# The row of D in a fused SSM-convolution and SwiGLU kernel: loaded through GpSimd's DMA queue instead of SyncE's

## The chip, the cores and the metric

One NeuronCore of a Trainium2 chip runs the whole kernel. The metric is the device time of one execution in microseconds (us), as the median of several. A profiled execution of the same program gives the trace; its times are microseconds from the start of the span unless marked otherwise. The engines are PE (TensorE, with PEld for its weight loads), DVE (VectorE), ACT (ScalarE), POOL (GpSimd) and SP (SyncE, which here only issues transfers). "SPq" marks the instruction that issues a transfer on SP's queue; transfers issued by POOL show as POOL instructions, since GpSimd spends its own time on them.

## The reference

The input has 2048 rows of 640 numbers. Two layers follow each other, both with a residual:

```python
kv = (sum of 4 shifted copies of k, each times a column of shift_k) * v
y  = causal convolution of kv with ssm_k, per channel (done by FFT of 2*S)
y  = y + kv * ssm_D
h  = x + layernorm(x) * y
h2 = h + (silu(n @ w_gate) * (n @ w_up)) @ w_down,   n = layernorm(h)
```

`ssm_D` is one row of 640 numbers. The product `kv * ssm_D` is the same as adding `ssm_D` to the first tap of the convolution kernel `ssm_k`, and so the kernel adds this row once, to one row of the first block of `ssm_k`.

## The kernel before

The sequence is cut into four blocks of 512 rows. For each block j the kernel does, in names that the code uses: load g (a block of `ssm_k`), k, v and x; turn g on PE (L471) and evict the result (L473); multiply the shifted k on PE (block 0: L639, the later blocks: L648) and multiply with v (kv); take the spectra X (of kv) and G (of g) by matmuls with the constant WF (L375), each result copied out of PSUM by ACT (L364) or DVE (L367) and completed by one subtraction on DVE (L410); multiply spectra on DVE (block 0: L719, stage "m00"); go back by an inverse transform (L878); multiply with the layernorm of x and add x (L892, L905); normalise, turn (hT) and run the feed-forward part (gate and up: L1022, down: L1110).

Nothing is left to a scheduler at run time. The function records every operation with its engine and its buffers in a `Plan`, and the list `ORDER` gives the order in which the recorded operations are written out; each number is the index of an operation, and a negative number `n` means operation `~n` on its other engine (a copy on DVE instead of ACT, or a load issued by POOL, called "pld", instead of SP). Each engine then runs its own operations in that order, and waits at each for what it needs. Buffers come from a few pools and are handed out in the same order (12 of "big", 5 of "row", 4 of "ps", which are the PSUM tiles). The list was made by a planner that is not part of the kernel.

The operations that matter for the change, with their numbers in `ORDER`:

- 22, 29, 26, 27, 28 and 205 are the first loads, all on SP: k (L597), g of block 0 (L330), x (L342), v (L337), WF (L1199), x of block 1 (L342). Each is 512 or 640 KB. Operation 31 is the load of the row of D (L1208), 1280 bytes into partition 0 of a "row" buffer; it is the seventh transfer on SP's queue.
- 63 is the addition of that row to the turned g, on DVE (L477). It stands in `g_turned`, behind the four evictions of the turned g (56, 58, 60, 62; L473). Operation 62 is the fourth of these.
- 44, 47 and 53 (L658) multiply three of the four products of k with v on DVE; 50 (ACT, L664) and 51 (DVE, L665) do it for the fourth.
- 64 to 97 are the spectrum X of block 0, in two halves of the columns; its pairs of matmuls are the even numbers 64, 66, ..., and their evictions the odd ones. 98 to 129 are G of block 0, which alone needs the sum made by operation 63. 142 is the first multiplication of m00.
- 13 (POOL, L1170) rearranges the taps once these have landed, 12 (POOL, L1166) writes one fifth of the diagonals for the product with k, 24 (POOL, L1189) clears a tail.
- 614 is a copy of the shifted k of block 3 inside SBUF (L563), issued by POOL. 533 is a load of weights for block 1's feed-forward part (L959). 290, 293, 296 and 299 are transfers by which POOL adds the four rows of block 1's result into x (L278). 307 is the last of the four normalisations of block 1 (L807), behind which the last transpose by DMA (L919) is issued.

Of the kernel before, what the change touches and what calls it, by code (L numbers as in the profile page):

```python
# [68 lines left out]
TW = PAD + BLK  # L69
CUTS = ("X0", "G0", "m", "i")  # L70
ORDER = [
# [36 lines left out]
SLOTS = {'S': 8, 'big': 12, 'kT': 0, 'tT': 1, 'row': 5, 'sg': 0, 'co': 2, 'ps': 4, 'sm': 6}  # L108
HOME = {t: "big" for t in ("scr", "x", "ld", "t4", "hT", "wgu", "diag")} | {"o": "row", "ps_c": "ps", "ps_f": "ps"}
SPLIT = ((0,), (1,))  # L110
# [102 lines left out]
def kernel(ctx: ExitStack, tc: tile.TileContext, A_q, A_k, A_v, A_shift_k, A_ssm_k, A_ssm_D, B_x,  # L213
          B_w_gate, B_w_up, B_w_down, out):
    nc = tc.nc
# [15 lines left out]
    plan = Plan(slots)  # L231

    def new(tag):
        return Buf(HOME.get(tag, tag), None, tag)
# [7 lines left out]
    def ap(b):  # L242
        if b.tag != "big":
            return b.ap if b.tag is None else place[b.tag][b.at]
        t = place["big"][b.at]
        return t if b.kind == "ld" else t.rearrange("p (k n) -> p k n", k=KT if b.kind in ("hT", "wgu") else 4 * KT if b.kind == "diag" else R)
# [17 lines left out]
    def load(nbytes, packet, fn, w, r=(), other=None):  # L264
        op = plan.moved("sp", nbytes, packet, fn, r, w)
        if other:
            op.other = ("pld", op.ns, other)
        return op
# [864 lines left out]
    def first(name):  # L1133
        plan.line(0, name)
# [70 lines left out]
        load(P * R * 4 * P * 2, 4096, lambda: nc.sync.dma_start(out=ap(minus)[:, 0:4, :], in_=minus_h.ap()), [minus])  # L1205
    first("Ld")
    drow = new("row")
    load(1280, 1280, lambda: nc.sync.dma_start(out=ap(drow)[0:1, :], in_=A_ssm_D.partition_broadcast(1)), [drow])  # L1208
    first("LWI")
    load(P * R * 4 * P * 2, 4096, lambda: nc.sync.dma_start(out=ap(WI), in_=wi_h.ap()), [WI])  # L1210

# [26 lines left out]
    for j in range(1, NB):  # L1238
# [4 lines left out]
        if j == 1:  # L1243
            stage("Lw")
            load(P * NC_FULL * D * 2, 1280, lambda: nc.sync.dma_start(
                out=ap(wd)[:, 0:NC_FULL, :], in_=B_w_down[0:NC_FULL * P, :].rearrange("(c p) d -> p c d", p=P)), [(wd, 0)])
# [84 lines left out]
```

## Time and profile before

| | |
|---|---|
| time, median of 3 runs | 263.84 us (263.32 to 264.68) |
| time of the profiled execution | 265.31 us |
| its span in the trace | 263.5 us |
| PE busy | 254.7 us (97%) |
| DVE, ACT, POOL busy | 201.3, 180.8, 96.3 us |
| transfers | 45.05 MB, 63505 packets |

The profiled execution took 265.31 us, of which the trace spans 263.5; the rest lies ahead of and behind the first and last instruction. The trace is read in four views: the page with its slices, the chain of waits (which work ended last, followed back), the waits themselves (who waited for whom), and the timeline, in which each row is a start, a duration, an engine, a line of the code, an operation with its tiles, and in brackets the idle time ahead of it with what ended it. A row with "xN" merges N instructions in sequence. The table of stretches gives each engine's busy time in a stretch, and the clock that PE was granted there, as a share of the full one.

### The profile page before, as it was taken

The page shows a single profiled execution, that of the slowest core. Times are in us where ns is not written, and L with a number is a line of the kernel's source. Part 1 is how long each engine was busy: PE and PEld are TensorE (multiplying, and loading weights), DVE is VectorE, ACT ScalarE, POOL GpSimd, SP SyncE. Part 2 cuts the span into 40 slices and gives each one's busy share as a digit, 9 for nine tenths or more (in the row PEclk, how much of TensorE's full clock was granted, in tenths as well). Part 3 has the DMA queues.
Part 4 walks back from the last instruction along what each step waited for, and adds up shares of the span by engine and source line. Part 5 has one row for each costly group of instructions (what it writes and reads, how often), then busy time and mean ns, then how long its engine had stood idle before and what let it go on. Part 6 is the DMA issues. An engine that isn't in the chain of part 4 may idle for free.

```text
span 263.5 us, 4713 instructions
## 1 busy us (share of the span) xinstructions
PE 254.7 (97%) x1818; PEld 155.7 (59%) x1818; DVE 201.3 (76%) x263; ACT 180.8 (69%) x295; POOL 96.3 (37%) x115
## 2 busy tenths in 40 slices
PE   8979989999999999999999999999999999999993
PEld 7946658654566467764465467544446764444662
DVE  4388999999999999999999999999998300002231
ACT  2858999999999896889877879174677035345100
POOL 6923900003932952582017790407942022000000
PEclk9989999999999999999999999999999999999999
DMA  6997979978998999996997957765869557000011
GB/s 212 397 256 182 256 158 346 212 189 243 248 284 126 147 215 209 197 200 136 230 239 156 243 131 149 150 102 124 187 199 279 92 149 96 0 0 0 2 50 50
DMA packets 63505, 45.05 MB, mean 171 GB/s; under 512 B 30966, under 2 KB 58940, under 8 KB 63484
## 3 DMA queue, kind: packets, MB, share of 16 engines
q1 hardware_dynamic: 57586, 32.30, 49.2%
q0 software_dynamic: 5888, 12.46, 25.2%
q8 instruction: 14, 0.23, 0.4%
q14 instruction: 7, 0.06, 0.1%
q10 hardware_dynamic: 10, 0.01, 0.0%
HBM read 30.01 MB, written 4.59 MB: 131 GB/s over the span
## 4 chain that ended last, share of the span: by engine, by line
PE 81%; DVE 9%; DMA 3%; ACT 3%; SPq 1%; issue 1%; DVEq 0%
PE ps L1022 44%; PE ps L1110 23%; PE ps L375 8%; PE ps L878 4%; DMA row<-in_A_ssm_D_dram 3%; DVE S L719 2%; PE ps L648 2%; ACT big L364 1%; DVE row L892 1%; DVE big L658 1%; DVE big L719 1%; ACT S L364 1%; SPq L342 1%; DVE big L823 1%; DVE S L367 0%
## 5 line engine op out<-in xcount | busy, mean ns | idle before, releaser
L1022 PE MATMUL ps<-big,big 128*128 128x512 bf16 x540 | 120.5, 379 | 0.0
L1022 PEld LDWEIGHTS <-big 128*128 128x128 bf16 x540 | 52.4, 98 | 59.7
L1110 PE MATMUL ps<-wd,tT 128*128 128x320 bf16 (+2 forms) x416 | 60.9, 299 | 0.6 <-DVE row L1127 0.6
L1110 PEld LDWEIGHTS <-tT 128*128 128x128 bf16 x416 | 40.6, 98 | 17.4 <-issue 0.9
L375 PE MATMUL ps<-big,WF 128*128 128x320 bf16 x240 | 40.9, 308 | 2.7 <-ACT row L796 1.3
L1014 ACT ACTIVATE tT<-ps 128x1024 bf16<-128x1024 f32 x24 | 24.5, 1029 | 17.4 <-PE ps L1022 17.4
L1012 ACT CAST co<-ps 128x1024 bf16<-128x1024 f32 x24 | 24.0, 1015 | 16.5 <-PE ps L1022 16.1
L747 DVE TENSOR_TENSOR S<-S,big 128x2560 bf16<-128x2560 bf16 x23 | 34.3, 1492 | 0.8
L746 DVE TENSOR_TENSOR big<-S,S 128x2560 bf16<-128x2560 bf16 x23 | 34.1, 1484 | 0.2
L375 PEld LDWEIGHTS <-WF 128*128 128x128 bf16 x240 | 23.9, 100 | 15.6 <-issue 4.2
L1016 DVE TENSOR_TENSOR tT<-tT,co 128x2048 bf16<-128x2048 bf16 x12 | 14.6, 1220 | 16.6 <-ACT tT L1014 11.6
L757 ACT ACTIVATE row<-big 128x640 bf16<-128x640 bf16 x32 | 23.5, 736 | 2.6 <-DVE big L905 1.0
L364 ACT CAST S<-ps 128x640 bf16<-128x640 f32 (+1 forms) x34 | 18.6, 598 | 3.0 <-PE ps L375 3.0
L807 ACT ACTIVATE row<-big,sm 128x640 bf16<-128x640 bf16 x21 | 19.4, 940 | 0.0
L1117 POOL DMA_DIRECT2D out_dram<-row x12 | 12.0, 1218 | 19.7 <-ACT row L1116 19.7
L364 ACT ACTIVATE big<-ps 128x640 bf16<-128x640 f32 (+1 forms) x24 | 15.9, 700 | 4.1 <-PE ps L375 4.0
L1039 DVE TENSOR_TENSOR tail<-tail,co 64x512 bf16<-64x512 bf16 x4 | 1.6, 410 | 18.0 <-ACT co L1038 18.0
L278 POOL DMA_DIRECT2D big<-row x8 | 7.0, 999 | 22.9 <-DVE row L892 18.8
L1116 ACT CAST row<-ps 128x640 bf16<-128x640 f32 x12 | 7.9, 696 | 10.6 <-PE ps L1110 10.2
L959 POOL DMA_DIRECT2D big<-in_B_w_gate_dram x10 | 10.4, 1040 | 10.1 <-DVE S L747 8.4
L278 POOL DMA_DIRECT2D S<-big x2 | 2.6, 1291 | 28.4 <-ACT row L757 19.6
L892 DVE SCALAR_TENSOR_TENSOR row<-row,ps 128x640 bf16<-128x640 bf16 x16 | 12.9, 818 | 0.1
(109 smaller groups left out, 347.0 us busy)
## 6 DMA issues: line engine op xcount, KB each, us to landing
big<-in_B_w_up_dram SPq DMA_DIRECT2D x17, 320.0 KB, 5.0
big<-in_B_w_gate_dram SPq DMA_DIRECT2D x14, 320.0 KB, 5.3
big<-in_B_w_gate_dram POOLq DMA_DIRECT2D x10, 320.0 KB, 5.0
big<-in_A_ssm_k_dram SPq DMA_DIRECT2D x4, 640.0 KB, 6.7
big<-in_A_q_dram SPq DMA_DIRECT2D x4, 640.0 KB, 6.3
big<-in_A_v_dram SPq DMA_DIRECT2D x4, 640.0 KB, 5.5
big<-in_B_w_up_dram POOLq DMA_DIRECT2D x7, 320.0 KB, 4.8
wd<-in_B_w_down_dram SPq DMA_DIRECT2D x1, 2080.0 KB, 11.9
```

Of the source, the lines that this page charges most:

```text
L364: (lambda: nc.scalar.activation(dst(), src(), ACT.Copy, scale=2.0)) if twice else (lambda: nc.scalar.copy(dst(), src())),
L375: nc.tensor.matmul(ap(ps)[:, h, 0:NH], w, ap(src)[:, r, h * NH:(h + 1) * NH], start=(first and i == 0), stop=(last and i == len(rs) - 1), ...
L746: nc.vector.tensor_mul(flat2(b), X.part(xs), H.part(hs))
L747: f(A.part(dst), A.part(dst), flat2(b))
L757: act(825, lambda r=r, junk=junk: nc.scalar.activation(ap(junk), ap(x)[:, r, :], ACT.Square, scale=D ** -0.5, accum_out=sm(s, 1)[:, r:r + ...
L807: nc.scalar.activation(ap(row), ap(x)[:, r, :], ACT.Identity, bias=sm(s, 5)[:, r:r + 1], scale=sm(s, 4)[:, r:r + 1])
L892: nc.vector.scalar_tensor_tensor(two(ap(t)), two(ap(t)), 1.0, half(ap(ps)), op0=ALU.mult, op1=ALU.mult, accum_out=sm(s, 0)[:, r:r + 1])
L1012: act(1010, lambda ps=ps: nc.scalar.copy(ap(co)[:, at:at + 2, :], ap(ps)), src, [(co, gi % 2)])
L1014: act(1010, lambda ps=ps: nc.scalar.activation(ap(tT)[:, c:c + 2, :], ap(ps), ACT.Silu), src, [done(range(c, c + 2), ROWS)])
L1016: dve(1220, lambda: nc.vector.tensor_mul(ap(tT)[:, c - 2:c + 2, :], ap(tT)[:, c - 2:c + 2, :], ap(co)), [co], [done(range(c - 2, c + 2), R ...
L1022: nc.tensor.matmul(ap(ps)[:, i, :], ap(w)[:, k, off:off + P], ap(hT)[:, k, :], start=(k == 0), stop=(k == KT - 1))
L1110: nc.tensor.matmul(ap(ps)[:, hf, to:to + n], t, ap(wd)[:, c, col + (hf - hs[0]) * NH:col + (hf - hs[0]) * NH + n], start=(c == order[0]), ...
```

## The change

The load of the row of D is issued by POOL. In the recorded plan it is a "pld" operation:

```diff
     first("Ld")
     drow = new("row")
-    load(1280, 1280, lambda: nc.sync.dma_start(out=ap(drow)[0:1, :], in_=A_ssm_D.partition_broadcast(1)), [drow])
+    plan.moved("pld", 1280, 1280, lambda: nc.gpsimd.dma_start(out=ap(drow)[0:1, :], in_=A_ssm_D.partition_broadcast(1)), [], [drow])
     first("LWI")
```

The planner's list was made anew for it, so the whole of `ORDER` differs. Its beginning:

```diff
 ORDER = [
-    23, 22, 0, 29, 2, 26, 4, 1, 5, 13, 6, 7, 10, 16, 14, 9, 8, 27, 37, 3, 12, 15, 28, -39, 11, 42, 35, 205, 33, 39, 36, 41, 31,
-    40, -35, 137, 57, 59, 366, 134, -61, 55, 43, 49, -59, 46, -57, 63, 132, 50, 30, -45, 51, 45, 133, 52, 136, 192, 197, 130, -48,
-    24, -54, 64, -66, 68, 69, 200, 21, 17, 199, 81, 198, 61, 135, 54, 48, 66, -63, 25, 82, -68, 70, 131, -72, 89, 83, 84, 195,
+    23, 4, 0, 1, 2, 5, 7, 6, 22, 31, 3, 39, 40, 8, 29, 13, 26, 27, 14, 15, 37, 38, 10, 24, 12, 9, 28, 11, 42, 33, 35, 41, 36, 57,
+    366, 55, -35, 43, 137, -57, 133, 205, 30, 192, -59, 134, 59, -61, 49, 50, 46, 132, -45, 51, 130, 52, -48, 136, 200, 45, -54,
+    54, 16, 64, 68, 48, 199, 81, 65, 82, 17, 198, -70, 20, 61, 66, -63, 70, 21, 135, 197, -68, -72, 89, 83, -91, 25, 131, 195,
...
```

In the instructions that this list gives, the load of D is the first transfer of POOL, ahead of operation 13, and is written there as sixteen pieces of 40 numbers; on SP it was one piece of 640. Operation 63 stands on DVE behind 53, 69, 62, 67, 71 and 90, where it stood ahead of 44 before. The number of matmuls is the same. Seven loads of weights go from SP to POOL (533, 759, 825, 826, 842, 860, 868) and eight from POOL to SP (550, 566, 741, 767, 833, 851, 859, 867); the copy 614 goes from POOL to SP as well. Three evictions of X go from DVE to ACT and three from ACT to DVE; one eviction of the turned k (38) and one normalisation (721) go from DVE to ACT, and one normalisation (515) from ACT to DVE. The rest of the list keeps the same operations in a similar order, with neighbours exchanged.

66 rows, old and new, of the table ORDER are left out of this document.

## The prediction

> **What bounds the kernel now.** I read the page first, then the chain of waits, then the table of stretches around the place that the chain names.
>
> ```profile
> span 263.5 us, 4713 instructions
> ...
> PEclk9989999999999999999999999999999999999999
> ```
>
> PE is busy for 97% of this span: whoever wants to shorten this kernel has to find the few microseconds in which PE idles or runs slowly. The row of the clock shows one dip, in the third slice of 6.6 us. The chain of waits (start, duration, what) begins there:
>
> ```profile
> 4.49 9.04 DMA row<-in_A_ssm_D_dram
> ...
> 13.63 0.06 DVE big L477
> 13.69 0.35 issue
> 14.04 0.80 DVE big L658
> 14.84 0.40 DVE big L665
> ...
> 26.16 0.82 DVE S L719
> ```
>
> The row of D is issued at 4.49 and lands 9.04 us later, at 13.53. DVE adds it (L477, operation 63) and only then starts the product of kv with v (L658). The view of the waits says what that cost DVE:
>
> ```profile
> DVE big L477 <- DMA row<-in_A_ssm_D_dram: 3.3, 1, 3.3
> ```
>
> The stretches show what it did to PE (busy us and instructions of PE, PEld, DVE, ACT, POOL; granted clock; share of the transfer engines; GB/s):
>
> ```profile
> 13.70:17.20 3.50, 1.76 (x13) 0.98 (x13) 3.41 (x6) 2.13 (x6) 0.00 (x0) 1.00 1.43 305
> 17.20:20.60 3.40, 3.40 (x14) 1.97 (x14) 2.17 (x5) 2.13 (x7) 2.09 (x6) 0.53 0.81 151
> 20.60:26.20 5.60, 5.54 (x44) 3.93 (x42) 4.96 (x11) 4.64 (x14) 1.73 (x5) 0.98 0.76 187
> 26.20:53.00 26.80, 24.97 (x262) 18.41 (x261) 26.32 (x52) 26.22 (x52) 7.54 (x7) 1.00 1.00 245
> 53.00:206.00 153.00, 152.97 (x1009) 88.07 (x1008) 150.24 (x158) 121.66 (x185) 71.12 (x68) 1.00 0.87 188
> ```
>
> From 13.7 to 17.2 PE waits for kv and is busy for half the time; then it runs for 3.4 us at a granted clock of 0.53, and DVE and ACT wait for it. From 20.6 to 53 DVE and ACT are full and set the pace. From 53 on PE has no gap, and DVE is full as well until 206. So PE has slack only ahead of 53, and what DVE and ACT gain early is handed to PE.
>
> **The change part by part.** *The load on POOL.* These rows of the timeline matter:
>
> ```profile
> 1.14 0.29 POOL L1141 TENSOR_SCALAR_AFFINE_SELECT ident<-ident 128x128 bf16<-128x128 bf16 x1 [0.24 <-DVE ident L1138]
> 3.15 0.62 POOL L1170 COPY row<-row 5x512 bf16<-5x512 bf16 x1 [1.72 <-DMA row<-in_A_shift_k_dram]
> ...
> 4.49 0.33 SPq L1208 DMA_DIRECT2D row<-in_A_ssm_D_dram  x1
> ...
> 9.10 4.63 PE L639 MATMUL ps<-big,T 128*128 128x128 bf16 x80
> ```
>
> POOL is free from 1.43 and idles 1.72 us until the taps land. The issue goes into that gap. The only transfers that POOL issues in this trace come later; the first of the two rows here is the widest set of them (min/median/max ns), the second the slowest transfer of the first 16 us (KB each, us to landing):
>
> ```profile
> L1117 POOL DMA_DIRECT2D out_dram<-row x12: 855/1075/1816, 102.2 to 217.1; - x12
> ```
>
> ```profile
> tT<-const_minus SPq DMA_DIRECT2D x1, 512.0 KB, 11.2
> ```
>
> The issue, begun at 1.43, ends between 2.3 and 3.25. The bounds of its cost are 0 (hidden in the gap) and 0.1 us; I take 0. If the taps landed at once the full 1.1 would fall on L1170, 12 and the fifth of the diagonals, which the product with k (L639) needs only after 9.1: still nothing. SP saves the issue of 0.33 us, for loads that nobody waits for at that time.
>
> No row shows a small transfer on POOL's queue beside SP's large ones. From below, it lands with its issue, at 2.3. From above, it takes the 11.2 of the constant `minus`, from 3.25, hence 14.5. Between these I need not choose, because of the next part.
>
> *Operation 63 moved on DVE.* It now stands behind 53, 69, 62, 67, 71 and 90. The rows by which I work out when that is:
>
> ```profile
> 15.17 1.53 DVE L658 TENSOR_TENSOR big<-ps,big 128x640 bf16<-128x640 f32 x2
> ...
> 20.38 0.49 DVE L367 TENSOR_SCALAR big<-ps 128x320 bf16<-128x320 f32 x1 [1.11 <-PE ps L375]
> 20.92 1.92 DVE L367 CAST S<-ps 128x320 bf16<-128x320 f32 x4
> ```
>
> ```profile
> 14.04:26.16 12.12, 10.64 (x67) 6.84 (x68) 10.16 (x21) 8.86 (x24) 3.77 (x10) 0.86 0.96 206
> ```
>
> PE ends the last product with k at 13.73 whatever DVE does. DVE, free since 13.63 − 3.3 = 10.3, does 60, 44, 51 and 47 in that time: 0.48 + 0.77 + 0.4 + 0.77 = 2.4 us of 3.4 (L658 takes 1.53 for two; for 60, an eviction, I take the 0.48 of the row of four). So 53 runs from 13.75 to 14.5, and five evictions at 0.48 end at about 16.9, when 63 comes. The row of D has landed by 14.5 at the latest. The wait of 3.3 is gone by the order alone, and the new queue gives it a margin of 2 us or more.
>
> *What that is worth at the start of m00.* Before, from 14.04 to 26.16, DVE took 12.12 us, 10.16 of them busy. Of this, 44, 51 and 47 (0.77 + 0.4 + 0.77 = 1.94) now lie ahead of 13.75, and 63 (14.04 − 13.63 = 0.41) comes in. If every wait inside stays, m00 starts at 13.75 + 12.12 − 1.94 + 0.41 = 24.34, a gain of 1.82. One wait is that of 1.11 at 20.38, for a PE at half clock. In the new order PE goes on at 13.75 with X instead of idling: the matmuls of which 13 were spread over 13.7 to 17.2 now stand close together, and I expect no dip of the clock. So I take this wait as gone: m00 at 23.23, **a gain of 2.93**. If all waits of the 12.12 went, 12.12 − 10.16 = 1.96, the gain would be 1.82 + 1.96 = 3.78. Lower end 1.82, upper end 3.78.
>
> The row above has the clock at 0.53 right behind a stretch in which PE was busy 1.76 of 3.5 us. [...]
>
> *Whether the gain reaches the end.* DVE and ACT hand it on: between 26.2 and 53 they idle 0.5 and 0.6 us. PE can take it: ahead of 53 it idles 1.74 + 0.06 + 1.83 and loses about 3.4 × 0.47 = 1.6 to the clock, 5.2 together. The loads do not move, so each must have margin. The tightest that I found is the shifted k of block 1:
>
> ```profile
> 25.93 1.64 POOL L563 DMA_DIRECT2D T<-T  x2 [3.88 <-ACT S L364]
> ...
> 41.34 1.47 PE L648 MATMUL ps<-pairs,T 128*128 128x64 bf16 x40
> ```
>
> ```profile
> T<-T POOLq DMA_DIRECT2D x2, 321.2 KB, 9.1
> ```
>
> ```profile
> 116.94 15.27 PE L1022 MATMUL ps<-big,big 128*128 128x512 bf16 x70
> ```
>
> The second is issued by 27.6, lands 9.1 later at 36.7, and is used at 41.3, now 38.4: 1.7 left. The exchanged evictions cancel. The copy 614 (block 3), put on SP behind block 1's four transposes, loses most of its lead. If ACT reaches the copy that needs it just as it is issued, ACT waits the 9.1 of its like; three free PSUM tiles of ten matmuls, 30 × 15.27 / 70 = 6.5 us of PE work, cover that, and PE loses 9.1 − 6.5 = 2.6 at most. I take 0, since the wait begins only if ACT is there first. The weights that change queues have more time than 5 us between the release of their buffer and their use; 0 taken.
>
> **The sum.** Against the profiled execution's own time: 265.31 − 2.93 = 262.4. That execution lies 1.5 above the median of the runs, 263.84; the same difference gives 260.9, and with the margins named at nothing I predict **261.0**.
>
> **The rivals.** *A. The clock halves again.* Evictions, not matmuls, limit the X stage, and PE may have holes while four PSUM tiles are passed round. Against it: the stretch 20.6 to 26.2 kept 0.98. If it does, the lower end holds: 263.84 − 1.82 = 262.0.
>
> *B. Given back to the loads.* For it: the transfer engines' share is 1.00 over 26.2 to 53, so loads cannot come earlier; if the whole chain ahead of 53 follows them, the gain is nil, 263.8. Against it: in that stretch no compute engine's wait names a load. With 614's 2.6 lost it is 261.0 + 2.6 = 263.6, and between half and all of the gain lost the middle is 263.1.
>
> *C. Slower: a weight load blocks POOL's queue.* In the new order 533 stands between the first of block 1's four adds and the other three, and must wait until DVE has finished with the buffer.
>
> ```profile
> POOL big L959 <- DVE S L747: 8.4, 1, 8.4
> ```
>
> ```profile
> 84.73 1.74 POOL L278 DMA_DIRECT2D big<-row  x2 [2.37 <-ACT big L457]
> ...
> 111.61 1.60 SPq L919 DMA_TRANSPOSE big<-row  x1
> ```
>
> ```profile
> big<-row SPq DMA_TRANSPOSE x4, 3.6
> ```
>
> Behind the adds come the sums, POOL's norm, the transposes, and PE's first matmul on block 1, the L1022 at 116.94. The last transpose lands at 111.61 + 3.6 = 115.2, 1.7 ahead of PE. A wait like the 8.4 would start when POOL is free, 2.37 ahead of the second add; the adds slip by 6.0, PE by 6.0 − 1.7 = 4.3, and the time is 263.84 − 2.93 + 4.3 = 265.2. It is slower than before from a wait of about 2.4 + 1.7 + 2.9 = 7 on, and by over 0.5% just above the 8.4. Against it: the buffer is freed by block 2's L665, which DVE's order puts ahead of the second L892, so that the wait should be that of the add itself.
>
> *D. The load does not come sooner.* The row shows 9.04 us for 1280 bytes behind six large loads. [...] As worked out, 63 comes at 16.9, so the time is 261.0 either way; only the cause would be the order and not the queue.
>
> **How the numbers follow.** Forecast 0.50 (with D inside it, 0.2), A 0.17, B 0.17, C 0.16. The forecast's own range is 260.1 (all inner waits gone, 263.84 − 3.78) to 262.0. 0.5% of 263.84 is 1.3 us, about what a measurement of this kernel can tell from no change: faster is below 262.5, slower above 265.2. The forecast, A and a little of B are faster: 0.67. The rest of B and some of C are within: 0.18. C beyond its point, and waits that I have not found, are slower: 0.15. For 8 in 10, about 0.06 may lie below 259.8 and 0.14 above 265.0.
>
> **What would show it.** The wait of L477 for the row of D is gone, and it starts near 16.9; the row lands long before. L658's last ends near 14.5, not 16.7. The stretch 17.2 to 20.6 has a clock of 1.00. The first L719 starts near 23.2. L648 at 38.5 and the first L1022 of the feed-forward part come about 2.9 earlier, with no wait for a load. If m00 starts at 23.2 but the end does not follow, the gain was given back, and the waits between 26 and 206 name where; if PE idles at 114, it is 533 or 614. If m00 starts at 24.3 with a clock dip, it is A.

## The result and the profile after

The kernel after takes **262.23 us** (median of 6, 262.14 to 262.56), the kernel before beside it 264.18 (263.32 to 264.78): the ratio is 0.9931, with a 95% interval of 0.9909 to 0.9953. In a second group it was 262.31 against 263.56, ratio 0.9951 (0.9932 to 0.9970). The predicted time was 261.0, with a range of 259.8 to 265.0, so the result lies inside the range and 1.2 us above the point. The profiled execution of after took 262.15 us, with a span of 260.3; that of before 265.31 and 263.5. So the two traces differ by 3.2 us, and the medians by 1.3 to 1.95: this gap is the first thing to explain.

The page of the kernel after:

```profile
span 260.3 us, 4687 instructions
...
PEclk9999999999999999999999999999999999999998
```

The dip of the clock is gone. The chain of waits no longer starts with D, and DVE is not in it at the start; its first transfer is that of WF, for the first matmul of the spectrum X:

```profile
2.91 10.26 DMA WF<-const_wf
...
13.21 0.99 PE ps L375 x6
```

The load of D lies where the list put it, in POOL's gap (first the timeline, then the view of the transfers: KB each, us from issue to landing):

```profile
1.50 0.72 POOL L1208 DMA_DIRECT2D row<-in_A_ssm_D_dram  x1
3.01 0.63 POOL L1170 COPY row<-row 5x512 bf16<-5x512 bf16 x1 [0.79 <-DMA row<-in_A_shift_k_dram]
...
10.64 0.82 DVE L658 TENSOR_TENSOR big<-ps,big 128x640 bf16<-128x640 f32 x1 [0.36 <-ACT row L796]
...
12.38 1.58 DVE L658 TENSOR_TENSOR big<-ps,big 128x640 bf16<-128x640 f32 x2
...
16.12 0.47 DVE L477 TENSOR_TENSOR big<-big,row 1x640 bf16<-1x640 bf16 x1
...
22.40 0.81 DVE L719 TENSOR_TENSOR S<-S,S 128x1280 bf16<-128x1280 bf16 x1
```

```profile
row<-in_A_ssm_D_dram POOLq DMA_DIRECT2D x1, 1.2 KB, 5.7
```

The row lands at 1.50 + 5.7 = 7.2 instead of 13.53. L477 runs at 16.12 without a wait, the first L658 starts at 10.64 instead of 14.04, and m00 (the first L719) at 22.40 instead of 26.16. The stretches:

```profile
13.70:17.20 3.50, 3.47 (x27) 2.26 (x26) 3.44 (x9) 3.45 (x12) 0.78 (x3) 1.00 1.53 296
17.20:20.60 3.40, 3.40 (x25) 2.16 (x24) 2.76 (x7) 3.33 (x10) 3.24 (x7) 1.00 0.78 151
```

PE is busy for 3.47 of the 3.5 us of which it idled through half before, and the clock behind it is 1.00, not 0.53. Up to here the trace of after has won 3.76 us. At the end two things look worse. First the chain, in the last block's feed-forward part:

```profile
237.89 0.03 ACT tail L1037
...
238.39 0.99 ACT co L1012
239.38 0.49 ACT co L1033
...
239.91 1.24 PE ps L1022 x5
```

and then the timeline there:

```profile
239.91 1.24 PE L1022 MATMUL ps<-big,big 128*128 128x512 bf16 x5 [0.98 <-ACT co L1033]
...
256.10 0.27 PE L1110 MATMUL ps<-wd,tail 128*128 128x256 bf16 x1
256.40 0.89 DVE L1127 TENSOR_TENSOR row<-ps,big 128x384 bf16<-128x384 f32 x2 [0.89 <-PE ps L1110]
```

PE idles 0.98 us, because the second half of a PSUM tile (operation 880) stands in the list behind the eviction of its first half (L1033), which ACT does late. Behind PE's last matmul, DVE has both additions L1127 left, 0.89 us. The same place of before:

```profile
258.42 1.58 PE L1110 MATMUL ps<-wd,tT 128*128 128x256 bf16 x13 [0.65 <-DVE row L1127]
259.84 0.27 PE L1110 MATMUL ps<-wd,tail 128*128 128x256 bf16 x1
260.15 0.43 DVE L1127 TENSOR_TENSOR row<-ps,big 128x256 bf16<-128x256 f32 x1 [1.78 <-PE ps L1110]
```

There the first addition stood ahead of PE's last part, PE waited 0.65 for it, and only 0.43 was left behind. These end pieces come from the new list, not from D: a kernel below that has the new list with D on SP has the same 0.98.

### The profile page after: what moved, and what is told of

It reads as the page before. It is cut to its first block, busy times and chain, and to the rows that moved or that the text cites. A ratio compares the mean times of both kernels' runs of the same rounds, so it can differ in the third digit from the quotient of the medians.

```text
span 260.3 us, 4687 instructions
## 1 busy us (share of the span) xinstructions
PE 251.7 (97%) x1802; PEld 154.4 (59%) x1818; DVE 199.8 (77%) x262; ACT 180.3 (69%) x296; POOL 102.3 (39%) x114
## 4 chain that ended last, share of the span: by engine, by line
PE 84%; ACT 6%; DMA 4%; DVE 3%; issue 1%; SPq 1%; DVEq 0%; ACTq 0%
PE ps L1022 44%; PE ps L1110 23%; PE ps L375 10%; PE ps L878 4%; DMA WF<-const_wf 4%; PE ps L648 2%; ACT S L364 2%; ACT big L364 1%; DVE row L892 1%; ACT big L473 1%; DVE big L905 0%; ACT co L1012 0%; PE ps L471 0%; DVE big L658 0%; ACT big L928 0%
## 5 line engine op out<-in xcount | busy, mean ns | idle before, releaser
L1022 PE MATMUL ps<-big,big 128*128 128x512 bf16 x524 | 119.3, 379 | 1.8 <-ACT co L1033 1.0
L1022 PEld LDWEIGHTS <-big 128*128 128x128 bf16 x540 | 52.5, 98 | 61.3 <-issue 1.3
L375 PE MATMUL ps<-big,WF 128*128 128x320 bf16 x240 | 39.1, 298 | 1.3 <-ACT big L364 1.0
L375 PEld LDWEIGHTS <-WF 128*128 128x128 bf16 x240 | 23.1, 97 | 13.0 <-issue 2.0
L364 ACT ACTIVATE big<-ps 128x640 bf16<-128x640 f32 (+1 forms) x23 | 15.3, 714 | 2.2 <-PE ps L375 2.2
L1185 POOL TENSOR_SCALAR pairs<-row,taps 128x64 bf16<-128x64 bf16 x20 | 13.9, 718 | 0.1
L775 POOL TENSOR_TENSOR sm<-sm 128x4 f32<-128x4 f32 x6 | 12.4, 2070 | 2.8 <-ACT row L796 2.6
```

Source lines behind the costliest of these rows:

```text
L364: (lambda: nc.scalar.activation(dst(), src(), ACT.Copy, scale=2.0)) if twice else (lambda: nc.scalar.copy(dst(), src())),
L375: nc.tensor.matmul(ap(ps)[:, h, 0:NH], w, ap(src)[:, r, h * NH:(h + 1) * NH], start=(first and i == 0), stop=(last and i == len(rs) - 1), ...
L1022: nc.tensor.matmul(ap(ps)[:, i, :], ap(w)[:, k, off:off + P], ap(hT)[:, k, :], start=(k == 0), stop=(k == KT - 1))
```

## The experiments

The theory at the start: the wait of L477 and the dip that follows from it are what the change removed, and either of its two means, the other queue or the later L477, is enough. The rivals: only the new list as a whole does it; only the earlier landing does it; the dip of the clock is all there is. All times are medians; the ratio to the kernel before in the same group stands behind, with its interval.

### The queue alone

The list of before, with D on POOL ahead of POOL's first rearrangement:

```diff
-    load(1280, 1280, lambda: nc.sync.dma_start(...), [drow])
+    plan.moved("pld", 1280, 1280, lambda: nc.gpsimd.dma_start(...), [], [drow])
-    ..., 4, 1, 5, 13, 6, ..., 36, 41, 31, 40, ...
+    ..., 4, 1, 5, 31, 13, 6, ..., 36, 41, 40, ...
```

> The list of before, with the load of D issued by POOL as its first transfer; nothing else moves, and L477 keeps its early place on DVE, ahead of the first L658. My theory is that only the wait of 3.3 us counted, and that the queue or the new place of L477, either of them alone, takes it away. By it the row lands at about 7.2, as in the kernel after, L477 starts when DVE is free at about 10.3 with no wait, the first L658 follows, the stretch 17.2 to 20.6 keeps a clock of 1.00, and the first L719 of m00 starts between 22.4 and 22.9 (22.40 in the kernel after, and at most the 0.41 of L477 more). The time is 1.5 to 2.5 us below that of before. The rival, that the gain comes from the new order (of which L477 is one part) and not from the queue, expects L719 near 26.2 and the time of before within 0.4 us.

261.11 us, 0.9895 (0.9868 to 0.9921). The timeline of DVE:

```profile
9.26 0.55 DVE L477 TENSOR_TENSOR big<-big,row 1x640 bf16<-1x640 bf16 x1
10.85 0.82 DVE L658 TENSOR_TENSOR big<-ps,big 128x640 bf16<-128x640 f32 x1 [1.04 <-DMA big<-in_A_v_dram]
...
21.98 0.82 DVE L719 TENSOR_TENSOR S<-S,S 128x1280 bf16<-128x1280 bf16 x1
```

No wait for D; what is late next is v, by 1.04. The gain, 2.6 us by the medians of its group, is a little above the 1.5 to 2.5 expected and larger than that of the change: the queue does it without the new list.

### The order alone

The list of before, D on SP, operation 63 alone moved:

```diff
-    ..., -57, 63, 132, 50, ..., 196, -91, 20, 76, ...
+    ..., -57, 132, 50, ..., 196, -91, 63, 20, 76, ...
```

> The list of before, in which the one operation L477 is moved on DVE behind the five evictions that follow the last L658; D stays the seventh load on SP and lands at about 13.5. By my theory (either of the two removes the wait) L477 starts at 16 to 17 without a wait, the first L658 comes at about 10.8 instead of 14.04, the first L719 at 22.4 to 23.2, and the time is 1.5 to 2.5 us below that of before, as with the queue alone: the queue is then only a margin. The rival, that the earlier landing is needed, expects a wait of L477 or of what is behind it, L719 above 24.5 and less than half of the gain.

261.84 us, 0.9918 (0.9889 to 0.9947). The timeline of DVE:

```profile
10.62 0.82 DVE L658 TENSOR_TENSOR big<-ps,big 128x640 bf16<-128x640 f32 x1 [0.39 <-DMA big<-in_A_v_dram]
...
16.64 0.47 DVE L477 TENSOR_TENSOR big<-big,row 1x640 bf16<-1x640 bf16 x1
...
22.69 0.82 DVE L719 TENSOR_TENSOR S<-S,S 128x1280 bf16<-128x1280 bf16 x1
```

The order alone is enough as well, so neither the rival on the earlier landing nor the one on the whole list holds.

### Both, and the new list with SP

Two kernels complete the table. The first has both edits above in the old list; the second is the new list with D back on SP, behind the six large loads:

```diff
-    plan.moved("pld", 1280, 1280, lambda: nc.gpsimd.dma_start(...), [], [drow])
+    load(1280, 1280, lambda: nc.sync.dma_start(...), [drow])
-    ..., 6, 22, 31, 3, ..., 133, 205, 30, ...
+    ..., 6, 22, 3, ..., 133, 205, 31, 30, ...
```

> The list of before, with D issued by POOL as its first transfer and L477 late on DVE: both parts of the change that bear on the wait, and nothing else of the new list. If each alone removes the same wait, the two together give no more than the queue alone: 261.1, within 0.4 us. If they added up (two waits of their own), it would be near 259.5 to 260.

261.24 us, 0.9918 (0.9894 to 0.9942): no more than the queue alone, as expected of two ways to remove one wait.

> The new list of the kernel after, with the load of D put back on SP behind the first six large loads. With L477 late by the list, the theory (either the queue or the late L477 is enough) expects no wait of L477, which starts at about 16.1, the first L719 near 22.4 to 23, and the time of the kernel after within 0.4 us. The rival, that the new list needs the earlier landing, expects a wait of L477 and 0.7 us or more above it.

262.20 us, 0.9948 (0.9932 to 0.9964), first L719 at 22.58, L477 at 16.54 without a wait. Within the new list the queue makes no difference. The kernel after, unchanged, ran beside these two:

> The kernel after once more, beside the others of this group on one chip. By the theory so far its new list costs, against the queue alone in the old list, 0.98 us at the eviction in the last block's gate and up and about 0.45 at the last two additions (L1127), both behind PE's last matmul there, and saves the 0.65 that PE waits for the first of these additions in the old list, and 0.3 ahead of the last block. So it should be 0.4 to 1.1 us above the queue alone (261.11 in the last group), at 261.7 to 262.3. The rival, that the two kernels are the same and the difference came from the chips, expects 261.1 to 261.4.

262.31 us, 0.9951 (0.9932 to 0.9970), above the queue alone's interval of 0.9868 to 0.9921, which comes from another group on another chip; both edits in the old list, in the same group as this run, took 261.24. The new list costs about 1 us against the queue alone. Of its 1.0 us in the traces (spans 260.3 and 259.3) nothing lies ahead of PE's last matmul, which ends at 256.37 in both; 0.47 is the second L1127, and the other 0.5, between the last addition and the end of the span, no run here explains. It is regular, though: the span ends 2.5 us behind the last addition in the four kernels with the old list and D on POOL, 2.9 in the six profiles with the old list and D on SP, and 3.0 with the new list, whichever queue has D.

### The clock alone

The kernel before, with 22 matmuls on a constant that fill PE's gap ahead of the first L375:

```diff
         for op in plan.schedule(ORDER):
+            if op is plan.ops[64]:
+                ones = nc.const_aps.tensor(1.0, [P, P], BF16)
+                for _ in range(22):
+                    nc.tensor.matmul(ap(op.bufs[-1])[:, 0, 0:P], ones, ones, start=True, stop=True)
```

> The kernel before, with 22 extra matmuls of 128x128 on a constant, whose result is overwritten, put on PE ahead of the first L375, in the 1.27 us in which PE waits for kv; D and L477 stay as they were. By my theory the halved clock of 17.2 to 20.6 is a consequence of the half idle stretch ahead of it. Then PE is busy for about 3.0 of the 3.5 us, the clock there is 0.9 to 1.00, DVE's wait of 1.11 goes, the first L719 starts near 25.05, and the time falls by up to 1.1 us where the executions of before have the dip. The wait of L477 stays 3.3. The rival, that the dip has another cause, expects 0.5 to 0.6 in that stretch and no gain, or a small loss.

263.61 us, 0.999 (0.9975 to 1.0006): no gain in the median. But the executions say more. Of 66 executions of before in these groups, 16 had a mean clock of 0.991 to 0.994 and took 264.55 to 265.11 us (median 264.81); the other 50 had 0.997 or more and took 263.17 to 264.30 (median 263.58). The profiled execution of before, clock 0.993, was one of the first kind. With the filling, none of 12 was below 0.998, and the longest took 264.15; with the share of before, 12 without a dip would come up 4 times in 100. The 60 executions of all kernels of this study in which L477 does not wait had none below 0.996. So the dip goes with the wait of L477, it costs 1.2 us, and it happens in one execution of four. That the half idle stretch is the step between the wait and the dip is likely, but rests on those 12 executions: the profiled one does not help, as its stretches and timeline show.

```profile
13.70:17.20 3.50, 3.50 (x53) 3.21 (x51) 2.98 (x6) 2.29 (x8) 0.00 (x0) 1.00 1.51 290
17.20:20.60 3.40, 3.36 (x24) 2.17 (x23) 3.09 (x8) 3.35 (x11) 1.56 (x4) 1.00 0.92 149
```

```profile
12.94 0.50 DVE L477 TENSOR_TENSOR big<-big,row 1x640 bf16<-1x640 bf16 x1 [1.73 <-DMA row<-in_A_ssm_D_dram]
```

The clock is 1.00, as expected. But the wait is 1.73, not the expected 3.3, and PE ends the product with k at 14.64, not at 13.73, so that its stretch would not have been half idle without the filling either.

### The kernel before once more

Nothing is edited.

> The kernel before, profiled once more. Of its 49 executions in the groups so far, 11 had a mean clock of 0.991 to 0.994 and took 264.66 to 265.11 us, the other 38 had 0.997 or more and took 263.2 to 264.3; the first profile, 0.993 and 265.31, is of the few. If the dip of the clock is not in every execution, this one has it with a chance of about 2 in 9. Without it I expect 263.2 to 264.3 us, a clock of 0.9 to 1.00 from 17.2 to 20.6, a wait of L477 of 1.5 to 3 us, and the first L719 at 24.3 to 25.2 instead of 26.16. The rival, that every execution has the dip and the times differ for another reason, expects 0.5 to 0.6 in that stretch at 263.5 too.

263.54 us, clock 1.00, first L719 at 23.94, a little ahead of what I expected. The stretches and the timeline of this execution:

```profile
13.70:17.20 3.50, 3.06 (x34) 2.16 (x32) 3.37 (x7) 3.50 (x12) 0.00 (x0) 1.00 1.50 294
17.20:20.60 3.40, 3.40 (x26) 2.37 (x25) 3.15 (x8) 2.95 (x10) 2.80 (x8) 1.00 0.78 156
```

```profile
3.09 0.29 PE L1158 MATMUL ps<-ident,row 5*128 5x5 bf16 x4 [0.18 <-DMA row<-in_A_shift_k_dram]
...
7.43 1.88 PE L1151 MATMUL ps<-const-bfloat16-1.0 128*128 128x128 bf16 x16
...
9.98 4.63 PE L639 MATMUL ps<-big,T 128*128 128x128 bf16 x80
...
12.90 0.48 DVE L477 TENSOR_TENSOR big<-big,row 1x640 bf16<-1x640 bf16 x1 [1.71 <-DMA row<-in_A_ssm_D_dram]
...
23.94 0.82 DVE L719 TENSOR_TENSOR S<-S,S 128x1280 bf16<-128x1280 bf16 x1
```

This is an ordinary execution: the wait is 1.71, not 3.3, and PE ends the product with k at 14.61, not 13.73. The stretch ahead of 17.2 is not half idle here, since PE is busy for 3.06 of its 3.5 us; so the 50 executions without a dip may simply be those in which PE is late. Against it the change wins 1.54 at m00, and 263.54 − 262.15 = 1.4 in all.

### PE's late start

That PE is later here raised a doubt: perhaps the change gains because PE is earlier in its executions. The next kernel takes away the gap of 0.18 us in PE ahead of L1158, by three matmuls more in the filling in front of it (L1151, matmuls on a constant that keep PE busy until data come), and leaves D where it was:

```diff
-WARMUP = (18, 16, 16)
+WARMUP = (21, 16, 16)
```

> The kernel before, with 21 instead of 18 matmuls in PE's first filling (L1151), so that PE does not idle for 0.15 to 0.23 us at 2.9 until the taps land; D and the list stay as they were. In all profiles so far PE runs at half its pace from the start, and reaches the full pace at 4.2 to 6.6 where this gap is absent and at 6.9 to 9.3 where it is there; the kernels with D issued early (by POOL or by SP) have no gap. A second theory has come out of this: the change gains because PE is faster earlier, and not by the wait of L477. By it, closing the gap alone gives the full pace ahead of 7.6, the product with k (L639) ends near 13, the first L719 starts at 22.4 to 23, and the time falls by 1 us or more. By the first theory the row of D, landing at 12.9 to 13.6, holds L477 and what follows it whatever PE does: the wait of L477 grows to 2.5 to 3.5 us, the first L719 starts at 23.9 or later, and the time is that of before within 0.4 us.

263.67 us, 1.0006 (0.9986 to 1.0026), beside 263.67 for before. The timeline:

```profile
6.95 1.10 PE L1151 MATMUL ps<-const-bfloat16-1.0 128*128 128x128 bf16 x16 [0.27 <-DVE T L614]
...
8.73 4.63 PE L639 MATMUL ps<-big,T 128*128 128x128 bf16 x80
...
12.92 0.48 DVE L477 TENSOR_TENSOR big<-big,row 1x640 bf16<-1x640 bf16 x1 [2.99 <-DMA row<-in_A_ssm_D_dram]
...
23.96 0.82 DVE L719 TENSOR_TENSOR S<-S,S 128x1280 bf16<-128x1280 bf16 x1
```

PE is 1.25 us earlier, the wait of L477 grows by 1.28, and L719 stays at 23.96. The second theory falls: while D is late, PE's earlier product is worth nothing; it only makes the wait longer. Four of the 12 executions have the dip, with a mean clock of 0.991 or 0.992 and 264.74 to 264.98 us. The profiled one took as long, 264.77, for another reason: its clock is 1.00 throughout, behind a stretch in which PE was busy for 2.44 of 3.5 us, and PE idles 1.09 us far behind m00, at the first L1022 on block 1:

```profile
13.70:17.20 3.50, 2.44 (x16) 1.42 (x17) 3.37 (x7) 2.57 (x8) 0.00 (x0) 1.00 1.43 291
```

```profile
116.40 1.89 PE L1022 MATMUL ps<-big,big 128*128 128x512 bf16 x8 [1.09 <-ACT big L364]
```

In this kernel, in the last one and in the next, L719 starts 11.0 to 11.1 us behind L477's start (12.92 and 23.96, 12.90 and 23.94, 12.22 and 23.32). Where nothing waits for D, it starts 8.8 to 9.3 us behind the end of the product with k (12.65 and 21.98 with the queue alone, 13.65 and 22.69 with the order alone, 13.10 and 22.40 after, 15.12 and 23.97 with D first on SP, below). In these profiles m00 begins at the later of these two.

### Issuer or place

D on POOL, but at the place that the load has in the list of before; and D on SP, but as its first transfer. The first has only the two changed lines of the load from the queue alone, and the list of before.

> The list of before word for word, with D issued by POOL at the place where the load stands in that list, behind two of POOL's preparations (L1185 and L1166): POOL's queue, but no early issue. POOL comes to it at about 8 to 10. If the issuer alone counted, the row would land 5.7 us behind the issue as in the kernel after, at 14 to 16, L477 would wait 3 to 5 us, and the time would be that of before or up to 2 us more (263.5 to 265.5): then the early place on POOL does it. If the row lands within 2 us of a late issue, the wait is gone and the time is near 261.1 to 262.

262.38 us, 0.994 (0.9919 to 0.9961): about half of the queue alone's gain, between the two cases. The timeline, and the landing:

```profile
6.48 0.77 POOL L1208 DMA_DIRECT2D row<-in_A_ssm_D_dram  x1
...
12.22 0.53 DVE L477 TENSOR_TENSOR big<-big,row 1x640 bf16<-1x640 bf16 x1 [2.06 <-DMA row<-in_A_ssm_D_dram]
```

```profile
row<-in_A_ssm_D_dram POOLq DMA_DIRECT2D x1, 1.2 KB, 5.7
```

My mistake was the time of the issue (8 to 10, it was 6.48). The 5.7 us from issue to landing are the same at 1.50 and at 6.48, against the 9.04 on SP at 4.49. So in the kernel after the row is early for two reasons, 3.3 us less from issue to landing and an issue 3 us sooner. The first goes with POOL's queue, but on it the row also travels as sixteen pieces instead of one, and no run here separates these two.

The second has only this exchange in the list:

```diff
-    23, 22, 0, 29, ..., 36, 41, 31, 40, ...
+    23, 31, 22, 0, 29, ..., 36, 41, 40, ...
```

> The list of before, with D still issued by SP but as its very first transfer, ahead of k; nothing else moves. If the place ahead of the large loads is what brings the row early, and not the issuer, it lands before 8 and L477 does not wait, and the time is that of the queue alone (261.1) to 0.4 us more, since each of the large loads is issued 0.33 us later. If only another engine's queue can bring the row early, it lands at 11 or later, L477 waits 1 us or more, and the time is above 262.5.

262.59 us, 0.9953 (0.9928 to 0.9978), and neither case: six executions at 261.57 to 261.95, six at 263.23 to 263.89. The profiled one is of the second kind:

```profile
5.62 2.32 PE L610 MATMUL ps<-ident,T 128*128 128x128 bf16 x20 [0.46 <-DMA T<-in_A_k_dram]
...
10.49 4.63 PE L639 MATMUL ps<-big,T 128*128 128x128 bf16 x80
...
11.73 0.48 DVE L477 TENSOR_TENSOR big<-big,row 1x640 bf16<-1x640 bf16 x1
```

L477 does not wait, so the early place on SP also brings the row in time; in this trace nothing moves before 1.6 us, and 16 GB/s between 1.6 and 2.0, which is 6400 bytes, as many as the taps (5120) and the row (1280) have together, so by this sum the bytes of the row have moved within 1.2 us of the issue at 0.80. But k, pushed back, arrives late for PE by 0.46, PE stays at about half its pace until near 9.8 (16 matmuls of L1151 take 1.91 us at 7.73), and its product ends at 15.12. In place of the wait for D there is one for k. POOL's queue has no such price: with the queue alone L610 starts at 4.74 without a wait for k. That the six faster executions are those in which PE is not late was not seen in a trace.

### The end of the kernel

In the kernel after, the second half of that PSUM tile ahead of the evictions:

```diff
-    ..., 881, 883, 887, 880, 894, ...
+    ..., 881, 880, 883, 887, 894, ...
```

> The kernel after, with one pair of operations exchanged in the list at the end of the last block's feed-forward part: the second half of the last PSUM tile of gate and up (five L1022) stands ahead of the two evictions (L1033, L1038) instead of behind them, so that PE need not wait for an eviction of the other half. Each engine's own order is the same. In the kernel after PE idles 0.98 us there. If this wait is what was given back, PE goes on without it and the time is 0.9 to 1.0 us below that of after (262.23), about 261.3, or 2.9 below before. The rival: the evictions come later by as much and the down projection waits for them instead; then the time is that of after within 0.2.

261.72 us, 0.9912 (0.9885 to 0.9938): 0.5 to 0.6 below the two measurements of the kernel after by the medians, 0.5 to 1.0 by the ratios, with intervals that overlap. The timeline of PE:

```profile
229.77 10.09 PE L1022 MATMUL ps<-big,big 128*128 128x512 bf16 x46
239.70 9.13 PE L1110 MATMUL ps<-wd,tT 128*128 128x320 bf16 x66
```

The idle time of 0.98 is gone, and the down projection starts at 239.70 instead of 240.99 (0.15 of this was won already at m00, which starts at 22.25 instead of 22.40). So in the trace this wait was on the path, and the change gave it back there.

The queue alone, with a PSUM tile of its own for the last part of the down projection:

```diff
-            other = new("ps_f") if last and LASTCUT == 3 else ps
+            other = new("ps_f") if last else ps
...
-                return [(other if to else ps, ...
+                return [(other if hs == (1,) else ps, ...
```

and likewise in the two functions below that use `other`.

> The queue alone in the list of before, and one change at the end: the last row block's second part (256 columns) of the down projection gets a PSUM tile of its own, so that PE no longer waits 0.65 us for DVE's addition of the first part (L1127). If that wait is on the path to the end, the time falls by 0.6 us, to about 260.5, and PE's last matmul ends 0.65 earlier. The rival: DVE's last addition and the last transfer are bound by something else behind it, and the time stays at 261.1.

260.29 us, **0.9873 (0.9855 to 0.9890)**, the fastest of all and clearly better than the kernel after; against the queue alone it is 0.6 us by the ratios and 0.8 by the medians of different groups, near the 0.6 expected, with intervals that overlap. The timeline:

```profile
253.82 1.58 PE L1110 MATMUL ps<-wd,tT 128*128 128x256 bf16 x13
...
255.55 0.42 DVE L1127 TENSOR_TENSOR row<-ps,big 128x256 bf16<-128x256 f32 x1 [0.97 <-PE ps L1110]
```

PE goes straight on; the idle 0.65 of before has no successor.

## Why the prediction was right or wrong

The account of the time, from the profiled executions (us):

| | before, with dip | before, once more | after | queue alone |
|---|---|---|---|---|
| first L719 | 26.16 | 23.94 | 22.40 | 21.98 |
| from there to the end of PE's last matmul | 233.95 | 234.38 | 233.97 | 234.39 |
| from there to the end of the span | 3.4 | 3.4 | 3.9 | 2.9 |
| span | 263.5 | 261.7 | 260.3 | 259.3 |

- **The load on POOL, cost nothing: right.** The issue of 0.72 lies in the gap, and L1170 starts at 3.01, ahead of the 3.15 of before. The landing at 7.2 was inside 2.3 to 14.5.
- **"The wait of 3.3 is gone by the order alone": right**, shown by the order alone. But that the queue gives only "a margin" undersold it: in the old list the queue removes the wait as well. Its gain was larger (261.11 against 261.84, with intervals that overlap); of the 1.2 us between the two traces 0.7 lies ahead of m00, where PE's product ended 1.0 earlier in the one than in the other, and 0.5 behind the last addition.
- **Rival D, that the load does not come sooner, did not happen**: 5.7 us on POOL's queue at both places, against 9.04 on SP's. For this transfer of 1.2 KB beside large ones that is 3.3 us less from issue to landing, with the sixteen pieces as the other possible cause.
- **L477 near 16.9: forecast 0.8 too late.** It came at 16.12, since PE ended the product with k at 13.10. "At 13.73 whatever DVE does" failed: this end lay between 12.65 and 15.12 in the profiles of this study.
- **The gain at m00, 2.93: the size was off.** Against the same trace it was 3.76, near the upper end of 3.78, but not because all waits went, as that end assumes. The stretch from the end of the product with k to m00, in the kernel after:

```profile
13.10:22.40 9.30, 9.16 (x68) 6.19 (x69) 8.37 (x19) 8.94 (x27) 4.77 (x11) 1.00 1.09 230
```

  DVE still idles 0.93 us in it, near the 0.85 that the forecast left. Of the 0.83 that the forecast missed, 0.63 is PE's product, which ended at 13.10 and not at 13.73, and 0.2 is less work of DVE.
- **No dip of the clock: right**, 1.00 from 17.2 to 20.6. The dip goes with the wait of L477 (16 of 66 executions of before, none of the 60 without the wait); that the half idle stretch brings it is likely, not shown. Rival A did not happen.
- **From the profiled execution to the median: the step that failed.** I took "the same difference", 1.5 us, off both. But the profiled execution of before was of the one in four with the dip, and 1.2 us of its gain do not exist in the others. It was also longer, at 265.31, than each of the 66. Against an ordinary execution the whole gain is 1.4. The 1.95 of the first comparison is larger because three of the six executions of before took 264.52 to 264.78 there, which is where those with a dip lie.
- **"What DVE and ACT gain early is handed to PE": right.** From m00 to PE's last matmul the kernel after needs 233.97, the one before 233.95 or 234.38. Rivals B and C did not happen, and neither did a loss by 614. But the margin of 1.7 us at the shifted k of block 1 was used up: its copy was issued at 27.64, and the weight load of L648 at 37.55 waits 0.26 us for it.
- **The end: a term that I had at nothing.** I looked for what the new list may lose only up to the first blocks' loads and queues, and called the rest "neighbours exchanged". It lost 0.98 at the PSUM tile (0.65 of it was won back where PE no longer waits for L1127) and 0.47 behind PE's last matmul.

So the forecast of 261.0 was 1.2 us low: 1.5 was taken off in going to the median that the kernel after does not have (its median and its profiled execution differ by 0.1), and 0.56 that the traces lose behind m00 (3.76 against 3.2) stood at nothing; the 0.83 by which the gain at m00 was set too low goes against them. The time is near rival A's 262.0, but not for its reason. And the 262.4 forecast for the profiled execution, which took 262.15, was met partly by luck: the gain at m00 was set too low, and the loss behind it left out.

What stays open: why PE reaches its full pace earlier in some executions, whether the executions without a dip had a half idle stretch at all, whether the queue or the sixteen pieces shorten the way from issue to landing, and the 0.5 us behind the last addition that separate the queue alone from the order alone and from the kernel after.

## What to carry to other kernels

Before a gain is taken from one trace to the median, ask whether that execution is an ordinary one: a clock row below those of the other runs, or a time above their range, says that part of what the change removes there is not in the others. A wait for a small load has three cures (another queue, an earlier place, a later use), and the cheapest is the one that pushes nothing back: here SP's first place made PE wait 0.46 us for k, and with the other queue PE did not wait for it. And when a list is written out anew for a small edit, read its end as closely as the place of the edit; here the edit alone in the old list was about 1 us better.

## What the runs showed of the hardware

- A row of 1.2 KB landed 5.7 us after its issue on POOL's queue, at 1.50 as at 6.48 (5.6 to 6.5 in seven profiles), and 9.04 us after it as the seventh on SP's. As the first on SP's its bytes had moved within 1.2 us of the issue, by the sum of 6400 bytes above.
- PE runs at about half its pace from the start, while the granted clock reads 1.00. In the execution of before shown above, 16 matmuls took 1.88 us at 7.43, where the same line takes 1.10 in the kernel without the gap, at 6.95. The stretches of that execution:

```profile
7.40:9.40 2.00, 2.00 (x24) 2.00 (x22) 0.36 (x2) 1.39 (x3) 2.00 (x6) 1.00 1.01 388
9.40:11.40 2.00, 2.00 (x40) 2.00 (x38) 1.29 (x3) 1.58 (x6) 1.88 (x5) 1.00 1.02 417
```

  24 and 40 matmuls in 2 us, at a clock of 1.00 in both. The change came between 4 and 10 us in the profiles of this study. Where PE did not wait for the taps near 3 us, these 16 matmuls took 1.10 at 6.08 to 6.95 in seven profiles, but 1.91 at 7.73 with D first on SP. The column of the granted clock does not show the change, and what sets its moment is not shown by a run here.
- The dip of the clock came in only 16 of 66 executions of one and the same program. In the profiles, a stretch with PE busy for 1.76 of 3.5 us had it behind it, stretches with 2.44 and 3.06 had not. Why it comes in some executions only is not shown by a run here.
